# Linear attention and MLP, two layers on one core: TensorE transposes, per-chunk sums of phi(K), one load line and a clock warm-up in the first attention half

## Chip, cores, metric

One core of a Trainium2 chip. The metric is the device time of one execution in microseconds (us), median of several. A profile gives the span of one execution, some 1.8 us less than its time. Engines: PE is TensorE (PEld its weight loads), DVE is VectorE, ACT is ScalarE, POOL is GpSimd, SP is SyncE, which issues transfers. The record calls an execution slow when it is over 1.5% above the fastest of the same kernel, and fast otherwise. Ratios and medians here are of fast executions.

## The reference

```python
def _A_ref(x, wqkv, wo):                      # B,S,D = 1,2048,512; H = 32 heads of 16
    q, k, v = split_heads(x @ wqkv)
    phi = lambda t: jnp.where(t > 0, t + 1, jnp.exp(t)) + 1e-6
    pq, pk = phi(q), phi(k)
    kv = jnp.einsum("bhsd,bhse->bhde", pk, v)
    z = jnp.einsum("bhsd->bhd", pk)
    num = jnp.einsum("bhqd,bhde->bhqe", pq, kv)
    den = jnp.einsum("bhqd,bhd->bhq", pq, z)[..., None] + 1e-6
    return merge_heads(num / den) @ wo
# ... _B_ref: layernorm, gelu(y @ w1 + b1) @ w2 + b2, F = 1792
x = x + _A_ref(_layernorm(x), A_wqkv, A_wo)
x = x + _B_ref(_layernorm(x), B_w1, B_b1, B_w2, B_b2)
# and both once more
```

kv and z are sums over all 2048 tokens. Nothing behind them can start before the last token tile has been normalised, transposed, multiplied and summed.

## The kernel before

Tokens lie in 16 tiles of 128, four to a chunk. The program is a graph of operations. When it is built, a list scheduler walks the graph, gives every engine a fixed order from priorities (`CONF`) and rough durations, and deals out buffers and PSUM banks. Each engine then runs its line strictly in that order, waiting on semaphores. A changed duration or operation can so change the order of everything.

A token tile of the first half: statistics, rstd by a power on POOL, the norm, the transpose by DMA, K, phi, and G = y' phi(K), held in four PSUM banks over all 16 tiles (V's weights are applied later, to G).

```python
G.op("dve", lambda e: e.bn_stats(stats[:, s.slot, :], src()), ...)                       # norm()
G.op("pool", lambda e: e.tensor_tensor(rstd..., veps..., neghalf[:], op=ALU.pow), ...)
G.op("dve", lambda e: e.tensor_scalar(yb[:, y.slot, :], src(), mv..., rstd..., ...), ...)
# ... transpose()
return e.dma_start_transpose(dst, yb[:, y.slot, :])                                      # on SP
# ... attn_k(): four matmuls, then phi() = exp and relu on ACT, min and add on DVE, and
G.op("pool", lambda e: e.tensor_tensor(zacc[:], zacc[:], pkb[:, pk.slot, :], op=ALU.add), 1060, ...)
# ... attn_kv(): z from zacc by four float matmuls, after all 16 tiles
```

Tokens and the K weights are loaded at once from two queues; later weights are each issued from POOL behind the transpose of some tile (tiles 3, 4, 6, 8, 10, 12).

Of the kernel before, what the change touches and what calls it, by code (L numbers as in the profile page):

```python
# [5 lines left out]
FP32 = mybir.dt.float32  # L6
# [4 lines left out]
P = 128  # L11
S = 2048
D = 512
# [97 lines left out]
class Scheduler:  # L111
# [13 lines left out]
    def run(self):  # L125
# [14 lines left out]
        dma_free = {e: 0.0 for e in ENGINES}  # L140
        left = len(g.ops)
        while left:
# [50 lines left out]
            if e == "sp" or o.sem is not None:  # L193
                begin = max(at + 100.0, dma_free[e])
                dma_free[e] = begin + o.nbytes
                o.end = dma_free[e] + o.lat
            else:
                o.end = at + dur + o.lat
# [83 lines left out]
def assign_waits(graph, order, sems, dma_sems):  # L282
# [10 lines left out]
    while len(done) < total:  # L293
# [45 lines left out]
    P_DEN=-26.42, P_A2=-18.03, P_W1=-20, P_W2=60.8, P_K=57.09, P_G=112.94, P_Q=209.56, STEP=4.23, A1_Q=54.88,  # L339
    A1_STEP=0.81, N_H=3, N_N=2, GAP=20.55, TABLE_PENALTY=28.66, WINDOW=199.3,  # L340
    SHIFT={
        "B00": -43.3, "B01": -114.4, "B02": -3.1, "B10": -64.2, "B11": -19.4, "B12": 0.1, "B13": 20.3,
        "D00": -0.8, "D01": -10.8, "D02": 12.4, "D03": -7.8, "D10": -47.3, "D11": -25.2, "D12": 14.0,
        "D13": -11.5, "G00": 37.6, "G01": -77.2, "G02": -29.0, "G03": -10.1, "G11": -54.7, "G12": 12.0,
        "G13": 2.7, "K00": -55.0, "K01": -125.9, "K02": 2.5, "K03": 5.1, "K10": -18.4, "K11": 18.2,
        "K12": -110.6, "K13": 7.6, "N00": -105.8, "N01": -6.7, "N10": -103.0, "N11": 102.7, "N12": 20.6,
        "N13": -61.5, "O00": -5.8, "O01": 9.2, "O02": -104.5, "O03": -191.9, "O10": -61.1, "O11": -27.2,
        "O12": -8.3, "O13": -95.1, "Q00": -5.3, "Q01": -8.6, "Q03": 3.2, "Q11": 7.5, "Q13": -17.6,
        "U00": -69.9, "U01": -24.5, "U02": -15.0, "U03": 4.7, "U10": -72.1, "U11": -2.2, "U12": -137.9,
        "U13": -0.4, "V0": 4.1, "V1": 1.7, "W00": 20.4, "W01": 9.8, "W02": 39.8, "W03": 14.4, "W10": 3.7,  # L350
        "W11": -12.6, "W12": 7.1, "W13": -1.0,
# [4 lines left out]
def build_kernel(nc, A_x, A_wqkv, A_wo, B_x, B_w1, B_b1, B_w2, B_b2, out, conf=None, report=False):  # L356
# [5 lines left out]
    with ExitStack() as es:  # L362
# [14 lines left out]
        id16 = SB("id16", [16, 16], BF16)  # L377
# [28 lines left out]
        def bank(t, n=512):  # L406
# [17 lines left out]
            "g4": ((0,), 1),  # L424
            "n": ((6, 7, 5, 4, 3, 2, 1, 0), cf["N_N"]),
# [6 lines left out]
        def dma(eng, fn, writes, tiles=(), reads=(), prio=0.0, name="", kb=0, sem=None, after=(), transpose=False):  # L432
            sem = sem or f"d_{name}"
            if sem not in dma_names:
                dma_names.append(sem)
            busy = 1300.0 if transpose else 100.0 + kb * 1024 / 230.0
            return G.op(eng, fn, 950.0 if eng == "pool" else 100.0, reads=reads, writes=writes, tiles=tiles, prio=prio,
                        name=name, lat=1000.0 if transpose else DMA_LAT, sem=sem, nbytes=busy, after=after)
# [6 lines left out]
        wsrc = A_wqkv.rearrange("(dt p) c -> p dt c", p=P)  # L445
        for k in range(4):
            dma("sp", lambda e, k=k: e.dma_start(x0ap(0, k), x_dram[k * P:(k + 1) * P, :]), [("x0", k)], [x0[0]],
                prio=-100 + k, name=f"x{k}", kb=128)
            if k == 0:
                dma("act", lambda e: e.dma_start(wqkv[:, :, D:2 * D], wsrc[:, :, D:2 * D]), ["wk"], prio=-99.5, name="wk", kb=512)  # L450
        for c in range(1, NC):
            dma("act", lambda e, c=c: e.dma_start(
                t4[:, x0[c].slot, :].rearrange("p (k d) -> p k d", k=4),
                x_dram[c * 512:(c + 1) * 512, :].rearrange("(k p) d -> p k d", p=P)),
                [("x0", 4 * c + k) for k in range(4)], [x0[c]], prio=-90 + c, name=f"xc{c}", kb=512)

        G.op("pool", lambda e: e.memset(neghalf[:], -0.5), 100, writes=["neghalf"], prio=-100)
        G.op("pool", lambda e: e.memset(eps6[:], 1e-6), 100, writes=["eps6"], prio=-97)
        wq_dma = dma("pool", lambda e: e.dma_start(wqkv[:, :, 0:D], wsrc[:, :, 0:D]), ["wq"], prio=-99, name="wq", kb=512)
        G.op("pool", lambda e: e.memset(ones32[:], 1.0), 100, writes=["ones32"], prio=-98)  # L460
        G.op("pool", lambda e: e.memset(id16[:], 1.0), 100, writes=["id16"], prio=-98)
        G.op("pool", lambda e: e.affine_select(id16[:], id16[:], pattern=[[1, 16]], compare_op=ALU.is_equal, fill=0.0,
                                               base=0, channel_multiplier=-1), 200, reads=["id16"], writes=["id16"], prio=-97)
        b1_dma = dma("sp", lambda e: e.dma_start(b1r[:], B_b1.rearrange("(ft p) -> ft p", p=P)), ["b1r"], prio=-80, name="b1", kb=4)
        dma("sp", lambda e: e.dma_start(b2b[:], bass.AP(B_b2.tensor, B_b2.offset, [[0, P], [1, D]])),
            ["b2b"], prio=-79, name="b2", kb=128)

# [3 lines left out]
        def consts(prio, after):  # L471
            G.op("pool", lambda e: e.memset(onesm[:], 1.0), 500, writes=["onesm"], prio=prio, after=after)
            G.op("pool", lambda e: e.affine_select(bdmask[:], onesm[:], pattern=[[0, DT], [-16, 8], [0, 16]],
                                                   compare_op=ALU.is_ge, fill=0.0, base=0, channel_multiplier=1),
                 900, reads=["onesm"], writes=["bdmask"], prio=prio)
            G.op("pool", lambda e: e.affine_select(bdmask[:], bdmask[:], pattern=[[0, DT], [16, 8], [0, 16]],
                                                   compare_op=ALU.is_ge, fill=0.0, base=15, channel_multiplier=-1),
                 900, reads=["bdmask"], writes=["bdmask"], prio=prio)
# [42 lines left out]

        def yTa(yT):
# [14 lines left out]
        def attn_k(L, c, k, yT, prio):  # L537
# [13 lines left out]
            phi(b, f"k{L}_{st}", lambda: pkb[:, pk.slot, :], f"pk{L}_{st}", [pk], prio, f"k{L}_{st}")  # L551
            if st == 0:
# [7 lines left out]
        def attn_q(L, c, yT, pq, prio):  # L560

            G.grp = f"Q{L}{c}"
            for kt in range(DT):
# [9 lines left out]
                phi(b, f"q{L}_{c}_{kt}", lambda kt=kt: yTa(pq)[:, kt, :], f"pq{L}_{c}_{kt}", [pq], prio + 0.8 * kt, f"q{L}_{c}_{kt}")  # L573

# [51 lines left out]
        def attn_kv(L, prio):  # L626

            G.grp = f"V{L}"
            zt = Tile(psum, f"zb{L}", "g")
            b = Tile(psum, f"kv{L}", "g")  # L630

            def zfn(e):
                for kt in range(DT):
                    ins = e.matmul(bank(zt)[:, kt:kt + 1], lhsT=zacc[:, kt * P:(kt + 1) * P], rhs=ones32[:, :], start=True, stop=True)
                return ins
            G.op("pe", zfn, 900, reads=["zacc", "ones32"], writes=[f"zp{L}"], tiles=[zt], prio=prio, name=f"Z{L}", lat=MM_DRAIN, n=8)

            def fn(e):
                for kt in range(DT):
                    for dc in range(DT):  # L640
# [6 lines left out]
                                                  bank(zt)[:, 0:DT].unsqueeze(2).broadcast_to([P, DT, P]), op=ALU.mult), 640,  # L647
                 reads=[f"zp{L}", "bdmask"], writes=["zb"], tiles=[zt], prio=prio, name=f"zb{L}", lat=40)
# [40 lines left out]
        def mlp_front(L, c, k, yT, prio, on_act):  # L689
# [3 lines left out]
            transpose(y, ykey, yT, k, f"yB{L}_{st}", prio, f"B{L}_{st}")  # L693
# [21 lines left out]
        def mlp_down(L, c, k, g, prio, last):  # L715
# [14 lines left out]
            else:  # L730
# [9 lines left out]
        G.op("pe", lambda e: e.matmul(bank(b1b)[:, 0:FT], lhsT=b1r[:, :], rhs=id16[0:FT, 0:FT], start=True, stop=True), 200,  # L740
             reads=["b1r", "id16"], writes=["b1p"], tiles=[b1b], prio=-60, name="b1T", lat=MM_DRAIN)
# [4 lines left out]
        for c in range(NC):  # L746
            yT = Tile(T4, f"yT0_{c}")
            pq = Tile(T4, f"pq0_{c}")
            pq1.append(pq)
            for k in range(4):  # L750
# [4 lines left out]
                tr = transpose(y, ykey, yT, k, f"yT0_{st}", pr, f"A0_{st}")  # L755
                pk = attn_k(0, c, k, yT, pr + 3)
                attn_g_held(0, st, k, y, ykey, pk, gb, pr + 6)
                if st == 3:
                    late("wv", "wv", wqkv[:, :, 2 * D:3 * D], wsrc[:, :, 2 * D:3 * D], pr, 512, [tr])
                if st == 4:  # L760
                    late("wo", "wo", wo[:], A_wo.rearrange("(dt p) c -> p dt c", p=P), pr, 512, [tr])
                if st == 5:
                    consts(pr, [tr])
                if st in (6, 8):
                    h = (st - 6) // 2
                    late(f"w1_{h}", f"w1_{h}", w1[:, 2 * h:2 * h + 2, :], B_w1.rearrange("(dt p) c -> p dt c", p=P)[:, 2 * h:2 * h + 2, :],
                         pr, 896, [tr])
                if st in (10, 12):
                    h = (st - 10) // 2
                    late(f"w2_{h}", f"w2_{h}", w2[:, 7 * h:7 * h + 7, :], B_w2.rearrange("(ft p) c -> p ft c", p=P)[:, 7 * h:7 * h + 7, :],  # L770
                         pr, 896, [tr])
            attn_q(0, c, yT, pq, -60 + A1S * (4 * c + 3) + cf["A1_Q"])
        attn_g_out(0, gb, -10)
        attn_kv(0, -10)
# [4 lines left out]
        for L in range(2):  # L779
# [35 lines left out]
            if L == 0:  # L815
                attn_kv(1, NC * PERIOD)
# [90 lines left out]
```

## Time and profile before

| | before |
|---|---|
| time, median of 3 (range) | 370.57 us (367.44 to 370.70) |
| span of the profile | 367.5 us |
| first K matmul / last G / first MLP-up matmul | 13.3 / 62.9 / 89.0 us |

Three rows of the page: first the busy time of each engine; then, with the span in 40 slices of 9.2 us, PE's busy share and its granted clock, each digit in tenths.

```profile
PE 325.9 (89%) x1468; PEld 145.6 (40%) x1497; DVE 224.9 (61%) x506; ACT 236.5 (64%) x364; POOL 121.1 (33%) x147
...
PE   0579478775999999999999999997999999998996
...
PEclk9999789996999999999999999998999999999999
```

PE's low digits and the low granted clock lie in the first ten slices: the first attention half and the way to the first MLP. By the working in the prediction they hold about three quarters of the loss, 38.9 of 51.1 us. I keep its names: stretch 1 is up to the first K matmul, stretch 2 from there to the last G, stretch 3 to the first MLP-up matmul, stretch 4 the rest.

### The profile page before, as it was taken

How to read it: one execution, taken by the hardware profiler on the slowest of the kernel's cores; microseconds unless marked ns; L12 is line 12 of the kernel's file. 1: busy time of each engine (PE TensorE's matmuls, PEld its weight loads, DVE VectorE, ACT ScalarE, POOL GpSimd, SP SyncE). 2: the span in 40 equal slices, each digit the busy share in tenths (PEclk: the TensorE clock that was granted, in tenths of full speed). 3: DMA queues.
4: the chain of work that ended last, by engine and by line, in shares of the span. 5: the costliest groups of instructions: out<-in, count | busy, mean ns of one | idle time of the engine just before them, and what ended most of it. 6: DMA issues, size and time to landing. Idle time of an engine off the chain costs nothing.

```text
span 367.5 us, 4243 instructions
## 1 busy us (share of the span) xinstructions
PE 325.9 (89%) x1468; PEld 145.6 (40%) x1497; DVE 224.9 (61%) x506; ACT 236.5 (64%) x364; POOL 121.1 (33%) x147
## 2 busy tenths in 40 slices
PE   0579478775999999999999999997999999998996
PEld 0233134331444444444444444442444444443442
DVE  2689797887089927684075769998852472361022
ACT  1445256986897999799924349896797468514600
POOL 2378573052045534173031534016610070070000
PEclk9999789996999999999999999998999999999999
DMA  8646990011012220021101120002110031021011
GB/s 255 159 128 159 174 226 2 0 30 29 0 30 43 43 45 15 14 45 28 29 3 29 29 45 14 0 4 57 31 28 29 0 85 31 0 71 45 0 45 43
DMA packets 41201, 18.77 MB, mean 51 GB/s; under 512 B 35356, under 2 KB 40092, under 8 KB 41180
## 3 DMA queue, kind: packets, MB, share of 16 engines
q1 hardware_dynamic: 37868, 11.15, 15.1%
q0 software_dynamic: 1200, 5.24, 4.8%
q10 hardware_dynamic: 2112, 2.10, 1.8%
q8 instruction: 12, 0.20, 0.2%
q14 instruction: 9, 0.07, 0.1%
HBM read 8.00 MB, written 2.10 MB: 27 GB/s over the span
## 4 chain that ended last, share of the span: by engine, by line
PE 67%; DMA 10%; DVE 9%; ACT 7%; POOL 4%; issue 2%; SPq 0%; DVEq 0%
PE ps L722 25%; PE ps L704 23%; DMA t<-yb 9%; PE ps L682 6%; PE ps L546 5%; PE ps L610 3%; DVE yb L508 2%; PE ps L568 2%; POOL rstd L496 2%; DVE eb L532 2%; POOL xsb L694 2%; ACT lr L667 1%; ACT gT L710 1%; PE ps L665 1%; DMA t<-in_A_x_dram 1%
## 5 line engine op out<-in xcount | busy, mean ns | idle before, releaser
L704 PE MATMUL ps<-t,w 128*128 128x512 bf16 x436 | 100.4, 383 | 2.0 <-DMA t<-yb 0.9
L722 PE MATMUL ps<-w,gT 128*128 128x512 bf16 x442 | 99.3, 379 | 0.7 <-ACT gT L710 0.3
L710 ACT ACTIVATE gT<-ps,b1c 128x512 bf16<-128x512 f32 x112 | 73.7, 688 | 21.9 <-PE ps L704 21.6
L496 POOL TENSOR_TENSOR rstd<-veps,neghalf 128x1 f32<-128x1 f32 x64 | 37.3, 588 | 143.4 <-DVE veps L490 104.9
L704 PEld LDWEIGHTS ps<-t,w 128*128 128x128 bf16 x448 | 44.0, 99 | 56.2 <-issue 2.7
L722 PEld LDWEIGHTS ps<-w,gT 128*128 128x128 bf16 x448 | 43.7, 98 | 53.5 <-ACT gT L710 0.8
L528 ACT ACTIVATE eb<-ps 128x512 bf16<-128x512 f32 x64 | 38.2, 601 | 34.5 <-PE ps L546 24.9
L532 DVE TENSOR_SCALAR eb<-eb 128x512 bf16<-128x512 bf16 x64 | 27.3, 428 | 35.5 <-ACT eb L528 34.9
L556 POOL TENSOR_TENSOR zacc<-zacc,pkb 128x512 f32<-128x512 f32 x30 | 36.2, 1206 | 36.3 <-DVE pkb L534 25.0
L546 PE MATMUL ps<-wqkv,t 128*128 128x512 bf16 x127 | 34.8, 412 | 13.4 <-DMA t<-yb 13.3
L694 POOL TENSOR_TENSOR xsb<-xsb,b2b 128x512 f32<-128x512 f32 x32 | 38.8, 1222 | 15.2 <-ACT yb L503 6.3
L530 ACT ACTIVATE rb<-ps 128x512 bf16<-128x512 f32 x64 | 38.4, 602 | 6.9 <-PE ps L546 6.9
L503 ACT ACTIVATE yb<-xsb,nmr,rstd 128x512 bf16<-128x512 f32 x24 | 19.4, 813 | 28.5 <-DVE nmr L500 28.5
L843 ACT ACT_TABLE_LOAD x28 | 35.9, 1283 | 0.5
L682 PE MATMUL ps<-gtb,t 128*128 128x512 bf16 x126 | 31.6, 394 | 4.9 <-DVE t L671 2.3
L485 DVE BATCH_NORM_STATS2 stats<-xsb 128x6 f32<-128x512 f32 x48 | 33.1, 690 | 0.9
L732 DVE TENSOR_TENSOR outb<-ps,xsb 128x512 bf16<-128x512 f32 x16 | 11.1, 691 | 34.0 <-PE ps L722 34.0
L568 PE MATMUL ps<-t,wqkv 128*128 128x512 bf16 x124 | 31.2, 387 | 0.2
L667 ACT ACTIVATE lr<-ps,eps 128x512 f32<-128x512 f32 x32 | 21.7, 677 | 8.2 <-PE ps L665 4.5
L671 DVE TENSOR_TENSOR t<-t,lr 128x512 bf16<-128x512 bf16 x32 | 22.3, 700 | 7.2 <-ACT lr L669 7.1
L686 DVE TENSOR_TENSOR xsb<-ps,xsb 128x512 f32<-128x512 f32 x16 | 10.7, 682 | 24.7 <-PE ps L682 24.7
L546 PEld LDWEIGHTS ps<-wqkv,t 128*128 128x128 bf16 x128 | 12.7, 104 | 32.2 <-DMA t<-yb 12.5
(54 smaller groups left out, 268.6 us busy)
## 6 DMA issues: line engine op xcount, KB each, us to landing
w<-in_B_w_dram POOLq DMA_DIRECT2D x4, 896.0 KB, 7.0
out_dram<-outb SPq DMA_DIRECT2D x16, 128.0 KB, 1.7
t<-in_A_x_dram ACTq DMA_DIRECT2D x3, 512.0 KB, 9.4
wqkv<-in_A_wqkv_dram POOLq DMA_DIRECT2D x2, 512.0 KB, 6.3
t<-yb SPq DMA_TRANSPOSE x64, 2.4
wqkv<-in_A_wqkv_dram ACTq DMA_DIRECT2D x1, 512.0 KB, 4.2
t<-in_A_x_dram SPq DMA_DIRECT2D x4, 128.0 KB, 5.7
wo<-in_A_wo_dram POOLq DMA_DIRECT2D x1, 512.0 KB, 3.8
```

What stands on the lines that cost most here:

```text
L496: G.op("pool", lambda e: e.tensor_tensor(rstd[:, s.slot:s.slot + 1], veps[:, s.slot:s.slot + 1], neghalf[:], op=ALU.pow), 570, reads=[k + ...
L528: G.op("act", lambda e: e.activation(eb[:, et.slot, :], bank(bt), ACT.Exp), 500, reads=[src_key], writes=[f"e{tag}"], tiles=[bt, et], prio ...
L530: G.op("act", lambda e: e.activation(rb[:, rt.slot, :], bank(bt), ACT.Relu), 500, reads=[src_key], writes=[f"r{tag}"], tiles=[bt, rt], pri ...
L546: ins = e.matmul(bank(b), lhsT=yTa(yT)[:, dt, k * P:(k + 1) * P], rhs=wqkv[:, dt, D:2 * D], start=(dt == 0), stop=(dt == DT - 1))
L556: G.op("pool", lambda e: e.tensor_tensor(zacc[:], zacc[:], pkb[:, pk.slot, :], op=ALU.add), 1060, reads=[f"pk{L}_{st}", "zacc"], writes=[" ...
L568: ins = e.matmul(bank(b), lhsT=wqkv[:, dt, kt * P:(kt + 1) * P], rhs=yTa(yT)[:, dt, :], start=(dt == 0), stop=(dt == DT - 1))
L682: ins = e.matmul(bank(wb), lhsT=yTa(pq)[:, kt, k * P:(k + 1) * P], rhs=gtb[:, kt, :], start=(kt == 0), stop=(kt == DT - 1))
L694: G.op("pool", lambda e: e.tensor_tensor(xsb[:, st, :], xsb[:, st, :], b2b[:], op=ALU.add), 1060, reads=[("x", st), "b2b"], writes=[("x", ...
L704: ins = e.matmul(bank(b), lhsT=w1[:, dt, ft * P:(ft + 1) * P], rhs=yTa(yT)[:, dt, :], start=(dt == 0), stop=(dt == DT - 1))
L710: G.op("act", lambda e, ft=ft, b=b: e.activation(gT[:, g.slot, ft * 512:(ft + 1) * 512], bank(b), ACT.Gelu_apprx_tanh, bias=b1c[:, ft:ft + ...
L722: ins = e.matmul(bank(b), lhsT=gT[:, g.slot, ft * 512 + k * P:ft * 512 + (k + 1) * P], rhs=w2[:, ft, :], start=(ft == 0), stop=(ft == FT - 1))
L843: e.preload_act_table_set(sets[table])
```

## The change

The intent: end the waits for DMA transposes by using TensorE for half of the first half's tiles, take the running sum of phi(K) off POOL, set all late loads into one line, and start TensorE's clock early. All priorities were fitted anew.

```diff
+        def transpose_pe(y, ykey, yT, k, key, prio, tag, on_act):   # 4 PE transposes into one PSUM bank, 1 copy on ACT
+                    ins = e.transpose(v()[:, d * P:(d + 1) * P], yb[:, y.slot, d * P:(d + 1) * P], idp[:])
...
-                tr = transpose(y, ykey, yT, k, f"yT0_{st}", pr, f"A0_{st}")
+                if st < cf["N_PT"]:                                  # 8: chunks 0 and 1
+                    tr = transpose_pe(y, ykey, yT, k, f"yT0_{st}", pr, f"A0_{st}", True)
+                else:
+                    tr = transpose(y, ykey, yT, k, f"yT0_{st}", pr, f"A0_{st}")
+                if st == 0:                                          # one line of loads behind tile 0
+                    load_chunk("pool", 2, -90, [tr])
+                    load_chunk("pool", 3, -89, [tr])
+                    late("wv", ...); late("wo", ...); late("w1_0", ...); late("w1_1", ...); late("w2_0", ...); late("w2_1", ...)
...
+        def attn_z(L, c, pks, prio):                                 # after each chunk; no sum on POOL in the first half
+                        ins = e.matmul(bank(b)[:, kt:kt + 1], lhsT=pkb[:, pks[k].slot, kt * P:(kt + 1) * P], rhs=onesm[:, 0:1], ...)
+                G.op("dve", lambda e: e.tensor_tensor(zs[:], bank(b)[:, 0:DT], zs[:], op=ALU.add), ...)
...
+        def warm(e):                                                 # 11 dead matmuls at the start
+                ins = e.matmul(bank(wu), lhsT=onesm[:, 0:P], rhs=onesm[:, :], start=True, stop=True)
...
-            transpose(y, ykey, yT, k, f"yB{L}_{st}", prio, f"B{L}_{st}")
+            if c < cf["N_PB"]:                                       # 1: chunk 0 of both MLP fronts
+                transpose_pe(y, ykey, yT, k, f"yB{L}_{st}", prio, f"B{L}_{st}", True)
...
-    P_DEN=-26.42, P_A2=-18.03, ...            # all priorities replaced; the scheduler's
+    N_PB=1, N_PT=8, P_DEN=-24.74, ...         # durations of loads and of transposes beside them too
```

## The prediction

> **What bounds the kernel now.** I began with the page: TensorE (PE) is 89% busy and the chain that ended last is 67% PE, so the time is PE's work plus PE's lost time. I then cut the span at three events of PE's own timeline: its first K matmul (13.3), the last G matmul of the first attention half (62.9; all 16 token tiles are summed there) and the first MLP-up matmul (89.0). This is the view of busy time in stretches (engine busy, in brackets instructions; then granted clock, DMA share, GB/s):
>
> ```profile
> core 0: us, PE busy (x) PEld busy (x) DVE busy (x) ACT busy (x) POOL busy (x), PEclk, DMA share, GB/s
> 0.00:13.30 13.30, 0.16 (x1) 0.10 (x1) 6.05 (x19) 2.75 (x3) 3.94 (x15) 1.00 0.91 272
> 13.30:62.90 49.60, 38.55 (x153) 15.87 (x157) 39.23 (x86) 23.91 (x46) 31.44 (x37) 0.93 0.62 132
> 62.90:89.00 26.10, 17.70 (x91) 7.97 (x90) 23.22 (x51) 21.97 (x40) 7.45 (x8) 0.93 0.10 21
> 89.00:367.50 278.50, 269.52 (x1226) 121.62 (x1249) 156.38 (x351) 187.90 (x278) 78.28 (x88) 0.99 0.13 29
> ```
>
> PE's busy time hides its losses, so I count weight loads (one per matmul; some matmul records are missing, no load is) and multiply by the pace of an unbroken run. Two lines of the chain of waits give the pace: 3.02 / 14 = 0.216 us for 512 columns, 0.89 / 16 = 0.056 us for 128.
>
> ```profile
> 146.10 3.02 PE ps L722 x14
> 237.54 0.89 PE ps L641 x16
> ```
>
> Work against length: stretch 1, about 0.2 of 13.3, 13.1 lost. Stretch 2, 156 x 0.216 = 33.7 of 49.6, 15.9 lost. Stretch 3, 67 x 0.216 + 0.9 (16 small ones) + 0.8 (the float sums of z) = 16.2 of 26.1, 9.9 lost. Stretch 4, 1225 x 0.216 + 1.7 = 266.3 of 278.5, 12.2 lost. So 316.4 us are work and 51.1 lost, 38.9 of it before 89.0. That is where the change works.
>
> What loses it, from the waits before 89.0 (engine, line, waited for: us in total, times, longest) and the chain of waits (start, us, what):
>
> ```profile
> PE ps L546 <- DMA t<-yb: 13.3, 5, 5.0
> PE ps L665 <- DVE t L534: 5.7, 1, 5.7
> ```
> ```profile
> 6.47 6.80 DMA t<-yb
> ...
> 38.51 4.85 DMA t<-yb
> ...
> 46.53 9.33 DMA t<-yb
> ...
> 82.77 1.37 DVE yb L508
> ```
>
> The reader is to see that PE stands for transposes by DMA of normalised tokens: 6.8 us for the first, 4.85 and 9.33 for two while weights load. In quiet stretches one lands in 2.4 us. The second limit is VectorE (DVE): 39 of 49.6 and 23 of 26.1 us busy. Part of that is not its own. Groups before 88 us by form (count | busy, mean ns):
>
> ```profile
> L532 DVE TENSOR_SCALAR eb<-eb 128x512 bf16<-128x512 bf16 x27 | 11.2, 417 | 6.4 <-ACT eb L528 6.2
> L534 DVE TENSOR_TENSOR pkb<-eb,rb 128x512 bf16<-128x512 bf16 x16 | 9.9, 621 | 1.1 <-ACT rb L530 0.7
> L508 DVE TENSOR_SCALAR yb<-t,mv,rstd 128x512 bf16<-128x512 bf16 x16 | 9.7, 617 | 2.8 <-POOL rstd L496 2.4
> L534 DVE TENSOR_TENSOR t<-eb,rb 128x512 bf16<-128x512 bf16 x11 | 8.1, 732 | 0.3
> L556 POOL TENSOR_TENSOR zacc<-zacc,pkb 128x512 f32<-128x512 f32 x15 | 17.4, 1159 | 7.3 <-DVE pkb L534 6.6 <-DVE veps L494 0.4
> ```
> ```profile
> 49.88 0.43 DVE L534 TENSOR_TENSOR pkb<-eb,rb 128x512 bf16<-128x512 bf16 x1
> ...
> 50.38 1.15 POOL L556 TENSOR_TENSOR zacc<-zacc,pkb 128x512 f32<-128x512 f32 x1 [1.35 <-DVE pkb L534]
> ...
> 50.54 1.28 DVE L534 TENSOR_TENSOR pkb<-eb,rb 128x512 bf16<-128x512 bf16 x1
> ```
>
> The same addition takes 0.43 us alone and 1.28 us under GpSimd's (POOL's) running sum of phi(K).
>
> **What the Trainium skill says.** (1) "SBUF — State Buffer", Who interferes with whom: DVE and GpSimd share one SBUF port pair as an exclusive lock, and a DVE op with two SBUF inputs blocks against a GpSimd op that reads SBUF. The 0.43 against 1.28 us agrees. (2) "TensorE: Matmul & The Clock Gate", What's actually happening: PE starts at half clock and needs about 3.4 us of activity to be released. The trace agrees: the first 16 matmuls took 5.49 us where 16 x 0.216 is 3.5, and the eight at 42.97 took 3.59 after 5 idle us. (3) The same page, Part 4: a PE transpose takes about 275 to 390 ns alone and lands in PSUM, so it must be copied out. No row of this trace has one; in a run of four I take the 56 ns of a 128-column matmul, an estimate. (4) "DMA: Bandwidth & Descriptors", Issuing engines are not separate DMA queues: all queues share 16 DMA engines. It agrees: transposes take 2.4 us in quiet and up to 9.3 beside weight loads.
>
> **The change part by part.**
> Transposes: tiles 0 to 7 of the first half, and the four of chunk 0 in each of the two MLP fronts, go to PE: 16 tiles x 4 x 0.056 = 3.6 us of PE, and 16 copies on ScalarE (ACT) at 0.6 (its PSUM reads of 512 take 0.60) = 9.6 us. ACT has room: 23.9 of 49.6 busy. A tile's path from yb to usable is about 0.4 + 0.6 + hand-overs, say 1.3 us, against 2.4 to 6.8. With yb 0 ready near 6.4, K 0 can start near 8 instead of 13.3: 5 us less lost in stretch 1.
>
> Loads: tokens of chunks 2 and 3 and all late weights (2 x 0.5 + wv 0.5 + wo 0.5 + 4 x 0.9 MB = 5.6 MB) are issued back to back from POOL once tile 0 is transposed, near 8 us. Eight issues x 0.85 (rows of 0.72 to 0.99) block POOL, and with it the rstd powers, until about 15. At the 330 GB/s that the DMA view shows in its fullest slices they land by about 26, so the DMA transposes of tiles 8 to 15 meet an idle fabric: 2.4 us each, not 4.85 and 9.33.
>
> Sums: 15 POOL additions and a cast, 18.0 us, go; 64 one-column matmuls come, bound by their weight loads at some 0.056 = 3.6 us, less the 0.8 of the old ones. DVE gets back: 27 minima x (0.417 - 0.29) = 3.4, 16 norms x (0.617 - 0.40) = 3.5, 16 x (0.621 - 0.43) + 11 x (0.732 - 0.43) = 6.4; together 13.3 us, most of it before 62.9.
>
> Clock: 11 warm-up matmuls x 0.427 = 4.7 us in idle time at the start, so the first K run goes at full clock: 5.49 - 3.5 = 2.0, and with no 5-us gaps the 1.9 at 43 is saved too.
>
> **Sum for stretch 2.** DVE needs per tile 0.61 + 0.21 + 0.15 + 0.38 for the norm and 0.70 for phi = 2.05, times 16 = 33 us, plus some six Q phis at 0.70 = 4, from 3.25 on with some 3 us of early gaps: 43. PE needs 128 x 0.216 = 27.6, transposes 1.8, sums 3.6, 24 Q matmuls 5.2: 38 from 8 on, 46 at best. Add some 4 us for the POOL block, which holds back tiles 2 and 3, and for handovers: the last G near 50 instead of 62.9, 13 us earlier. Stretch 3 is a chain (G copies, KV, M, copies, denominators, four norms with 1.16 us bias additions and 0.55 us powers on POOL): I shorten it from 26 to 24, for PE transposes and the early z; the first MLP-up matmul comes near 74. That is 15 off. Stretch 4 pays some 1.1 for transposes. The new priorities may fill part of its 12.2 lost us, such as the wait at 330 to 334 for the last chunk's transposes, or open others; I credit nothing net but the 1.1. So I take 15 off 370.6 for 355.6, and shade to 355 for the filling.
>
> **Rivals.** First: DVE stays the bound and the loss only changes its releaser. For it: DVE is busy 23 of 26 us in stretch 3, where no running sum blocks it, and 4 Q tiles per chunk remain. Against: 13.3 us of DVE time in stretch 2 are pure blocking. It would give about 7 off, 363. Second: the load burst moves the wait. POOL is held for 7 us, rstd comes late, x tiles 8 to 15 and wv arrive behind each other, and PE waits at 10 to 17 us as long as before. For it: POOL is in order and the burst stands ahead of the powers. Against: only tiles 2 to 7 are touched, and DVE has statistics to do meanwhile. It costs 5 of the 15: 360. Third: the schedule later absorbs it. MLP of chunk 0 starts early, but norms, Q and denominators of later chunks are not ready and PE gaps open at 75 to 100; for it, ACT is busy at 0.84 in stretch 3 and switches tables at 1.28 us each. It would leave 8 off, 362. Fourth, upward: the PE floor. 316.4 + 3.6 + 2.8 + 1 of handovers is 324; with 8 us of start, 12.2 late and only 6 elsewhere, the kernel would take 350 of span, 352 timed, and with the late gaps filled 346.
>
> **Range and chances.** The three ways down end at 360 to 363, the way up at 346 to 352; each change removes a measured loss from the chain, and none adds over 4 us to PE. Eight in ten: 346 to 362. Two per cent is 363.2. Faster 0.90, within 0.08, slower 0.02.
>
> **What would show it.** Right: first K matmul at 7 to 9 us; longest PE wait for a transpose under 3 us; the DVE additions of phi at about 0.43 in the first half; the granted clock 1.00 up to the last G, near 50; the first MLP-up matmul at 71 to 77; stretch 4 as long as before within 4 us. Wrong: a new PE wait on ACT copies or on rstd at 9 to 17 us; phi still slow, so that POOL's sum was not the cause; the first MLP-up at 74 but a span over 362, which would mean that the gain was given back later.

## The result

| | before | after |
|---|---|---|
| time, medians | 369.0 us (4 runs) | 356.65 us (4 runs) |
| ratio | | 0.9664 (0.9597 to 0.9731) |
| profiled span | 367.5 | 353.8 |
| stretch 1 | 13.3 | 7.1 |
| stretch 2 | 49.8 | 49.0 |
| stretch 3 | 25.9 | 18.6 |
| stretch 4 | 278.5 | 279.1 |

A ratio is the mean time of one kernel's fast runs over that of the other's of the same rounds, so it is not quite the ratio of the medians. In this table and below the last G is taken at the end of its last matmul, 63.1 before. The changed kernel was run again as a control on another chip: 0.9666.

The same rows of the page, after:

```profile
PE 332.0 (94%) x1628; PEld 150.1 (42%) x1628; DVE 216.0 (61%) x511; ACT 239.4 (68%) x376; POOL 103.2 (29%) x131
...
PE   6786998969989998999999999999999999999996
...
PEclk9998999989999999999999999999999999999999
```

Busy time in stretches, cut at the changed kernel's own events:

```profile
0.00:7.06 7.06, 4.86 (x16) 1.83 (x16) 2.96 (x8) 1.92 (x3) 3.38 (x13) 1.00 0.75 226
7.06:55.90 48.84, 40.84 (x254) 18.94 (x254) 34.22 (x107) 31.26 (x59) 14.71 (x23) 0.97 0.56 154
55.90:74.70 18.80, 13.77 (x84) 6.50 (x83) 16.83 (x37) 16.80 (x33) 6.98 (x8) 0.98 0.01 1
74.70:353.80 279.10, 272.57 (x1276) 122.83 (x1276) 162.02 (x361) 189.46 (x284) 78.11 (x89) 1.00 0.12 27
```

The total came as predicted, 356.65 us for 355, and so did the first MLP-up matmul, 74.7 for "near 74". (The saving is smaller than predicted, 12.4 us by the medians for 15.6: the prediction started from 370.6, the median of three, and four runs put the kernel before at 369.0.) But stretch 2 is hardly shorter, and stretch 3 gave what stretch 2 did not. Two errors cancelled, and the experiments are about them.

What filled stretch 2 is in PE's timeline (start, length, engine, line, instruction, count, idle time before and its releaser) and in one line of the chain of waits:

```profile
24.26 0.54 PE L630 MATMUL ps<-onesm,pkb 128*128 128x1 bf16 x16
29.87 1.89 PE L591 MATMUL ps<-wqkv,t 128*128 128x512 bf16 x4 [5.07 <-DMA t<-yb]
31.55 5.24 PE L647 MATMUL ps<-pkb,yb 128*128 128x512 bf16 x20
```
```profile
20.80 9.03 DMA t<-yb
```

Tile 8 is the first whose transpose is still a DMA. It was issued at 20.80, while the load line was running, and landed at 29.87, 9.03 us later; the last of the line's loads was issued at 16.2 and landed 12.4 us later, at 28.6. PE stood 5.07 us, and the first K group behind the gap took 1.89 us instead of 1.04: the clock had fallen.

DVE's groups in the first 75 us show that the sums no longer block it:

```profile
L577 DVE TENSOR_SCALAR eb<-eb 128x512 bf16<-128x512 bf16 x25 | 8.1, 328 | 6.2 <-ACT eb L573 6.1
L579 DVE TENSOR_TENSOR pkb<-eb,rb 128x512 bf16<-128x512 bf16 x16 | 6.7, 423 | 1.5 <-ACT rb L575 1.2
L529 DVE TENSOR_SCALAR yb<-t,mv,rstd 128x512 bf16<-128x512 bf16 x16 | 6.6, 422 | 1.3 <-POOL rstd L517 0.9
```

The additions went from 621 to 423 ns, the norms from 617 to 422, the minima from 417 to 328.

Stretch 3 in two pieces, cut at the first output projection (72.83 before, 62.26 after). First before, then after:

```profile
62.90:72.83 9.93, 7.81 (x51) 4.16 (x51) 9.24 (x20) 9.45 (x19) 0.00 (x0) 1.00 0.00 0
72.83:89.00 16.17, 9.89 (x40) 3.81 (x40) 13.98 (x31) 12.52 (x22) 7.45 (x8) 0.89 0.16 33
```
```profile
56.10:62.26 6.16, 4.66 (x34) 2.45 (x34) 5.63 (x13) 6.13 (x13) 0.00 (x0) 1.00 0.00 0
62.26:74.70 12.44, 8.92 (x51) 4.05 (x50) 11.00 (x26) 10.47 (x20) 6.98 (x8) 0.97 0.01 2
```

DVE and ACT are nearly full in the first piece in both kernels. After, they have 13 and 13 instructions in it instead of 20 and 19. PE's timeline shows five denominator matmuls (z times phi(Q)) between 48.8 and 55.1, before the last G; before the change the first came at 66.3, after it.

### The profile page after: what moved, and what is told of

It is laid out like the page before. It is cut to its first block, busy times and chain, and to the rows that moved or that the text cites. A ratio compares the mean times of both kernels' runs of the same rounds, so it can differ in the third digit from the quotient of the medians.

```text
span 353.8 us, 4505 instructions
## 1 busy us (share of the span) xinstructions
PE 332.0 (94%) x1628; PEld 150.1 (42%) x1628; DVE 216.0 (61%) x511; ACT 239.4 (68%) x376; POOL 103.2 (29%) x131
## 4 chain that ended last, share of the span: by engine, by line
PE 58%; DVE 11%; issue 10%; POOL 7%; ACT 7%; DMA 6%; ACTq 0%; DVEq 0%; POOLq 0%
PE ps L795 22%; PE ps L777 22%; DMA t<-yb 4%; PE ps L591 4%; PE ps L752 4%; POOL rstd L517 4%; DVE yb L529 3%; POOL xsb L767 3%; DVE stats L506 3%; PE ps L615 2%; PE ps L677 2%; DMA t<-in_A_x_dram 2%; ACT gT L783 2%; ACT lr L737 2%; ACT yb L524 2%
## 5 line engine op out<-in xcount | busy, mean ns | idle before, releaser
L783 ACT ACTIVATE gT<-ps,b1c 128x512 bf16<-128x512 f32 x112 | 74.6, 687 | 27.0 <-PE ps L777 26.7
L767 POOL TENSOR_TENSOR xsb<-xsb,b2b 128x512 f32<-128x512 f32 x32 | 38.6, 1210 | 16.2 <-ACT yb L524 9.8
L591 PE MATMUL ps<-wqkv,t 128*128 128x512 bf16 x128 | 32.4, 387 | 7.8 <-DMA t<-yb 6.0
L575 ACT ACTIVATE rb<-ps 128x512 bf16<-128x512 f32 x64 | 39.2, 612 | 0.0
L577 DVE TENSOR_SCALAR eb<-eb 128x512 bf16<-128x512 bf16 x64 | 20.4, 320 | 24.7 <-ACT eb L573 24.5
L741 DVE TENSOR_TENSOR t<-t,lr 128x512 bf16<-128x512 bf16 x32 | 23.5, 738 | 8.5 <-ACT lr L739 8.5
L603 POOL TENSOR_TENSOR zacc<-zacc,pkb 128x512 f32<-128x512 f32 x15 | 18.0, 1201 | 24.1 <-DVE pkb L579 22.0
L529 DVE TENSOR_SCALAR yb<-xsb,mv,rstd 128x512 bf16<-128x512 f32 x24 | 18.0, 748 | 7.0 <-POOL rstd L517 6.2
```

The costliest lines, as they stand in the source:

```text
L575: G.op("act", lambda e: e.activation(rb[:, rt.slot, :], bank(bt), ACT.Relu), 500, reads=[src_key], writes=[f"r{tag}"], tiles=[bt, rt], pri ...
L591: ins = e.matmul(bank(b), lhsT=yTa(yT)[:, dt, k * P:(k + 1) * P], rhs=wqkv[:, dt, D:2 * D], start=(dt == 0), stop=(dt == DT - 1))
L767: G.op("pool", lambda e: e.tensor_tensor(xsb[:, st, :], xsb[:, st, :], b2b[:], op=ALU.add), 1060, reads=[("x", st), "b2b"], writes=[("x", ...
L783: G.op("act", lambda e, ft=ft, b=b: e.activation(gT[:, g.slot, ft * 512:(ft + 1) * 512], bank(b), ACT.Gelu_apprx_tanh, bias=b1c[:, ft:ft + ...
```

## The experiments

Most experiments hold the order: each engine runs the operations that both versions have in exactly the order of the kernel that it is compared with, and a new operation gets the place of the one it stands for. Without this, the scheduler would reorder the whole kernel, and stretches 3 and 4 would move for other reasons. Buffers and PSUM banks are dealt anew. In the traces, the instructions of DVE and ACT come in the same order as in the kernel compared with, but for the added and removed ones. All twelve runs gave correct results. Lines of code (L...) differ between versions; the operation names do not.

### A control: the changed kernel again

The second group of runs, on another chip, has its own control, the changed kernel with no edit.

> The changed kernel once more, as the control for the other three on the same chip: 0.966 of the time before, within 0.005; last G at 55 to 57, first MLP-up matmul at 74 to 76 us.

Measured: 357.64 us, ratio 0.9666 (0.9614 to 0.9719), as expected; last G 57.0, first MLP-up 75.6, stretch 3 18.6 again. Its granted clock was 0.66 from 10 to 15 us, where the first profile had lost none, and 0.50 from 30 to 35 us, behind tile 8's wait, where the first had 0.69. So where and how far the clock drops varies from one execution to another; the last G of the two profiles differs by 0.9 us.

### GpSimd's sums put back, beside TensorE's

```diff
             if L == 0:
+                G.op("pool", lambda e: e.tensor_tensor(zacc[:], zacc[:], pkb[:, pk.slot, :], op=ALU.add), ...)   # result unused
                 return pk
```

> The changed kernel with every engine's order held, and the 16 running sums of phi(K) put back on GpSimd as dead work (nothing of the first half reads them; TensorE still makes the sums). It gives back the port lock alone. My theory: phi additions of the first half rise from 0.42 to over 0.6 us and minima from 0.33 to over 0.4, the last G of the first half slips from 55.9 to 59 to 62, and the span grows by 3 to 6 us. Rival: VectorE has slack in that stretch (34 of 49 us busy), so the additions are slower but the last G and the span move by less than 1.5 us.

Measured: 365.49 us, ratio 0.9938; last G 64.1 instead of 56.1, stretch 3 18.8, stretch 4 280.1. The cost is 0.9938 - 0.9664 = 0.027 of the time before, some 10 us, more than I expected. DVE's groups:

```profile
L749 DVE TENSOR_TENSOR pkb<-eb,rb 128x512 bf16<-128x512 bf16 x16 | 10.1, 635 | 0.3
...
L699 DVE TENSOR_SCALAR yb<-t,mv,rstd 128x512 bf16<-128x512 bf16 x16 | 8.0, 497 | 8.5 <-POOL rstd L687 8.1
```

Additions at 635 ns: the block is back. But DVE also idles 8.1 us for rstd instead of 0.9, because the powers stand behind the sums in POOL's line. Two costs, and the next experiment parts them.

### GpSimd kept as busy, without reading

The edit is shown against lock_back:

```diff
-                G.op("pool", lambda e: e.tensor_tensor(zacc[:], zacc[:], pkb[:, pk.slot, :], op=ALU.add), ...)
+                G.op("pool", lambda e: e.memset(scratch[:], 0.0), ...)      # 128x1260 bf16: 1164 ns
```

> As lock_back, but GpSimd's dead work only writes (a store of about the same length, which reads nothing that VectorE's additions need). It keeps GpSimd's line as full and takes away the block on two-input additions. lock_back put the last G at 64.1. If the time went through GpSimd's own line (rstd powers behind the sums), last G stays at 60 to 64; if it went through blocked additions on VectorE, phi additions are back at 0.42 us and last G at 56 to 58.5.

Measured: 359.34 us, ratio 0.9734 beside the control's 0.9666 in the same rounds.

```profile
L748 DVE TENSOR_SCALAR eb<-eb 128x512 bf16<-128x512 bf16 x24 | 10.3, 432 | 1.2 <-ACT eb L744 1.1
L700 DVE TENSOR_SCALAR yb<-t,mv,rstd 128x512 bf16<-128x512 bf16 x16 | 7.2, 451 | 9.0 <-POOL rstd L688 8.7
L750 DVE TENSOR_TENSOR pkb<-eb,rb 128x512 bf16<-128x512 bf16 x16 | 6.6, 417 | 0.6 <-ACT rb L746 0.3
```

The additions are free again at 417 ns while POOL is as full, and the waits for rstd stay (8.7 us). The minima, which have one input, are still slowed: 432 against 328. By the times, the full line, with the minima that its stores slow, costs 0.0068 x 370 = 2.5 us, and the reading some 7.5 of the 10. The 7.5 compares two groups of rounds, but the intervals are far apart (0.9857 to 1.002 for lock_back, 0.9680 to 0.9788 here). The 2.5 is likely and not certain: the control's interval, 0.9614 to 0.9719, overlaps this one, though only one of its six times is above the fastest here. By the profile the parts look more even (last G 61.4), but the profiled run was the slowest of its six, 362.15 us, so I go by the times: the blocked additions are shown to count, and they count more.

### No warm-up

```diff
-        G.op("pe", warm, 11 * 427, reads=["onesm"], ...)
```

> The changed kernel, order held, without the 11 warm-up matmuls. My prediction's step says 2.0 us of stretch 2: the first K matmuls run at half clock, some 0.43 us each, and the last G slips by 1 to 2 us. Rival: TensorE waits for VectorE and for data between 7 and 18 us anyway, so slower matmuls there only eat waits: last G and span within 0.7 us.

Measured: 352.93 us over the three fast runs (a fourth, 357.5, was slow), ratio 0.9586; last G 54.3, earlier than with the warm-up. Neither theory said that. The timeline has the reason:

```profile
29.62 1.04 PE L759 MATMUL ps<-wqkv,t 128*128 128x512 bf16 x4 [2.43 <-DMA t<-yb]
30.50 4.48 PE L815 MATMUL ps<-pkb,yb 128*128 128x512 bf16 x20
```

Without the warm-up everything up to tile 8 is later, and its transpose is issued at 23.19 instead of 20.80. It lands at 29.62 instead of 29.87: it seems to wait for the end of the load line either way, whose last load lands at 28.3 here and at 28.6 there. PE stands 2.43 us instead of 5.07, the clock holds, and the K group takes 1.04 us and the next twenty matmuls 4.48, where the changed kernel took 1.89 and 5.24. The warm-up saved its two microseconds and lost them at the load line, with the clock on top. The intervals of 0.9586 and 0.9664 overlap, so I claim no more than that it brought nothing here.

A caution on the clock column: in this run it reads 1.00 up to 15 us, though the K groups at 6.91 and 11.52 took 1.89 us each. Near the start, the matmuls' own times are the surer sign.

### Tiles 0 to 7 by DMA again

```diff
-    N_PB=1, N_PT=8, ...
+    N_PB=1, N_PT=0, ...         # and the load line starts behind the norm of tile 0, so at the same place
```

> The changed kernel, order held, tiles 0 to 7 of the first half transposed by DMA again (chunk 0 of the MLP fronts stays with TensorE); the late loads start at the same place as in the changed kernel. My theory: the transposes run beside the load burst, take 4 to 9 us each, first K near 12, several TensorE waits of 3 us and more, last G 6 to 12 us later than 55.9, span 6 to 10 us longer. Rival: VectorE sets the pace and catches up: first K late, but last G within 2 us.

Measured: 372.9 us, ratio 1.013 (1.006 to 1.020), a little slower than the kernel before. First K 10.5, last G 74.2 (18 us later, where I expected 6 to 12), stretch 3 18.6, stretch 4 278.6. PE's waits before 95 us:

```profile
PE ps L761 <- DMA t<-yb: 23.2, 7, 11.3
```

Seven waits, 23.2 us in all, the longest 11.3; one transpose took 18.3 us to land. The rival, that DVE sets the pace, falls. The load line without the transposes by TensorE costs 0.047, some 17 us. Whether the line pays at all beside them is not shown; the next experiment, which moves most of it, is faster.

### w1 and w2 issued after the last transpose of the half

```diff
-                if st == 0: ... late("w1_0", ..., [tr]) ... late("w2_1", ..., [tr])
+                if st == ST - 1: late("w1_0", ..., [tr]) ... late("w2_1", ..., [tr])   # tr: transpose of tile 15
```

> The changed kernel, order held but for this: the four loads of w1 and w2 (3.6 MB of the 5.6 MB burst) are issued only after the last DMA transpose of the first half has landed. My theory: the wait of 5.07 us for tile 8 and the half clock after it come from the burst; the transpose then lands in 2.4 to 4 us, the wait falls under 2 us, last G comes 4 to 6 us earlier (50 to 52) and the first MLP-up matmul 3 to 5 us earlier. Rival: stretch 3 is set by VectorE and ScalarE (16.8 of 18.8 us busy each), so an earlier last G only lengthens it: first MLP-up within 1.5 us of 74.7, span within 1.5 us.

Measured: 351.81 us, ratio 0.9559 (0.9488 to 0.9629; this touches the changed kernel's 0.9597 to 0.9731, but its times, 350.74 to 352.79, all lie below 355.55 to 357.47); last G 52.8, first MLP-up 71.4, stretch 3 18.6 again. PE's waits for transposes fall from 5.1 to 0.2 us; the longest landing is 4.0 us:

```profile
PE ps L761 <- DMA t<-yb: 0.2, 1, 0.2
```

The edit also takes 3.5 us of issuing out of POOL's line, ahead of the rstd powers. That is not where the gain comes from: from the first K matmul to the last z sums before tile 8 no_warmup takes 19.7 us and the run without warm-up below, with the loads moved, 19.6.

The rival falls: an earlier last G is passed on whole. But this profile lost its clock at another place, in the gap after the first K group (10 to 15 us, the columns as above, clock third from the end):

```profile
10.00:15.00 5.00, 4.25 (x15) 1.77 (x16) 4.62 (x17) 1.76 (x4) 3.29 (x6) 0.50 0.94 337
```

### The same without warm-up, and with more of it

```diff
-        G.op("pe", warm, 11 * 427, reads=["onesm"], ...)      # on top of the edit of the loads above
```

> late_w12 without the warm-up matmuls. My reading of no_warmup: the warm-up does save 2.4 us up to tile 8, but that is waited away at the load burst, which ends near 30 us either way; and the longer wait then drops the clock. With the burst moved, the warm-up should be worth 1 to 3 us again: last G at 53.5 to 56 against 52.8. But late_w12's own profile shows half clock from 10 to 15 us, warm-up or not, so if the clock falls in that gap anyway the two are within 0.7 us (rival).

Measured: 351.14 us, ratio 0.9502 (0.9459 to 0.9545); last G 51.7. So even with the loads out of the way, eleven warm-up matmuls brought nothing that can be told from noise: late_w12's interval is 0.9488 to 0.9629. The profiled executions suggest why: with the clock lost again, late_w12's K group at 11.47 took 1.89 us, as long as the one at 11.16 without a warm-up.

And with dead matmuls in two more places, the first warm-up kept:

```diff
+                    # dead matmuls on TensorE: 7 behind the first K group, 2 behind tile 1's transposes
+                    G.op("pe", bridge, 1.0, reads=["onesm"], ...)
```

> late_w12 with nine more dead matmuls on TensorE: seven in its idle time after the first K group (8.3 to 9.7 us), two behind the second tile's transposes. They keep the clock up in the gap where late_w12 lost it. Theory: granted clock 1.00 to the last G, tile 8 reached 2 to 3 us earlier, last G 50 to 51.5, span 348 to 349.5. Rival: VectorE's pace takes over (its norms and phi are busy 16 of 18 us there), last G within 1 us of 52.8.

Measured: 349.5 us, ratio 0.9463 (0.9418 to 0.9509), the fastest version; its profile:

```profile
6.75:50.30 43.55, 41.42 (x263) 19.24 (x263) 33.78 (x107) 31.43 (x60) 14.73 (x23) 1.00 0.55 174
```

The clock is 1.00 to the last G at 50.3 and stretch 2 is 43.6 us with PE busy 41.4 of them. Beside the control of the same rounds (0.9666) the loads and the filling together are worth 2%. Against late_w12_no_warmup alone the gain is 0.4% with overlapping intervals: a likely gain, not a shown one.

### Chunk 0 of the MLP fronts by DMA again

```diff
-    N_PB=1, N_PT=8, ...
+    N_PB=0, N_PT=8, ...
```

> The changed kernel, order held, with the transposes of chunk 0 of both MLP fronts by DMA again. Stretch 3 (last G to first MLP-up) was 25.9 us before and is 18.6 now; I had given it 24. My reading: 2.5 to 4 of those 7.3 us are this part, since from the end of the last normalised tile to the first MLP-up matmul it took 4.9 us before and takes 1.1 now. Expected: last G unchanged, stretch 3 at 21 to 22.5 us, span 3 to 6 us longer with the second layer's. Rival (all of stretch 3 is the new priorities): stretch 3 within 0.7 us of 18.6.

Measured: 361.14 us, ratio 0.9797, so this part is worth 0.013, or 4.8 us by the times (0.9753 to 0.9841, clear of the changed kernel's interval). It is spread thinner than expected: stretch 3 is 20.0, only 1.4 more, and stretch 4 is 281.6, some 2.5 more (the second layer). The last G was 58.4 in this profile, 2.3 later, from a wait of 6.8 us for tile 8's transpose, which the edit does not touch. PE's waits, for tile 8 and before the first MLP-up matmul:

```profile
PE ps L761 <- DMA t<-yb: 6.8, 1, 6.8
PE ps L947 <- DMA t<-yb: 6.3, 1, 6.3
```

My reading, that the fronts make up 2.5 to 4 us of stretch 3's gain, falls, and so does the rival, that they make up nothing. What is left, some 6 of 7.3 us, goes with the order; no run isolates it.

### Parts alone in the kernel before

```diff
+            attn_z(0, c, pks, pr + 6)     # sums of phi(K) by TensorE; POOL's out (its memset of ones goes to DVE)
```

> The kernel before, its order held, with one part alone: sums of phi(K) by TensorE per chunk. If GpSimd's sums were what set the time (lock_back cost 8 to 10 us), last G comes 4 to 8 us earlier than 63.1. If the waits for DMA transposes (13.3 us) set it, VectorE's gain is waited away and last G is within 2.5 us. Stretch 3 stays at 25.9 within 1 us.

Measured: 369.26 us, ratio 1.0007. The first half did gain: last G 58.8 (4.3 us earlier), first MLP-up 84.3 instead of 89.0, stretch 3 25.5. Stretch 4 gave it all back, 282.8 for 278.5. ACT's timeline and PE's show where the largest part of it went:

```profile
94.33 1.28 ACT L1050 ACT_TABLE_LOAD   x1
95.63 0.60 ACT L706 ACTIVATE eb<-ps 128x512 bf16<-128x512 f32 x1
96.24 1.28 ACT L1050 ACT_TABLE_LOAD   x1
```
```profile
98.28 1.78 PE L907 MATMUL ps<-t,w 128*128 128x512 bf16 x4 [2.87 <-ACT gT L913]
```

PE's next group for the MLP waits 2.87 us for a gelu that stands behind a pair of table loads around one exp. In the kernel before the same exp stood in the same place of ACT's line and no such wait is in the trace. As banks were dealt anew, the group may wait for another gelu than it did, so I do not claim that every insertion of this part would lose there. What is shown is that a gain in the first half reaches the end only if the order behind it can take it.

The same with tiles 0 to 7 transposed by TensorE as well:

```diff
-                tr = transpose(y, ykey, yT, k, f"yT0_{st}", pr, f"A0_{st}")
+                if st < 8:
+                    tr = transpose_pe(y, ykey, yT, k, f"yT0_{st}", pr, f"A0_{st}", True)
+                else:
+                    tr = transpose(y, ykey, yT, k, f"yT0_{st}", pr, f"A0_{st}")
```

> The kernel before, its order held, with two parts: sums by TensorE and tiles 0 to 7 transposed by TensorE; loads, warm-up, MLP fronts and priorities as before. My sum for stretches 1 and 2 was 13 us for all parts; these two should bring most of it: first K at 8 to 9, last G at 50 to 56, span 356 to 361. Stretch 3 stays at 25.9 within 1 us, since its gain came from the new order and the fronts. Rival (the new priorities and the load line matter most): last G later than 59.

Measured: 369.82 us, ratio 1.0033; first K 12.0, last G 59.4, stretch 3 25.5, stretch 4 282.8. My expectation failed. The held order was the reason for the late first K: PE's line begins with the transpose of b1, which waits 10.6 us for its load, and PE's transposes stand behind it. Waits for DMA transposes did fall, to 3.1 us, but the additional PE transposes brought nothing over before_z, and the rest gave back the same 4.3 us.

### The new priorities alone in the kernel before

```diff
-    P_DEN=-26.42, P_A2=-18.03, ...
+    P_DEN=-24.74, P_A2=-36.03, ...
```

> The kernel before with the new priorities alone: every engine's order is worked out again from them. Both sets of priorities were fitted to their own kernels, so I expect no gain: 0.98 to 1.04 of the time before. If the priorities by themselves carried the change, it is below 0.98.

Measured: 385.84 us, ratio 1.0452, somewhat outside the range I gave. The new priorities are worth nothing by themselves. Stretch 3 is 28.0 in its profile, so they do not shorten that alone either, although three denominators run before the last G here too (at 69.4 and 70.8, the last G at 72.0). Two of the parts on the old order give 1.00, the new priorities on the old parts 1.045, and both together 0.966.

## Why the prediction was right, and where its steps were not

- **Start.** "K 0 can start near 8": 7.1. The mechanism is right, for some 3.4 of the 6.2 us: dma_transposes puts the first K at 10.5. The other 2.8 came with the rest of the change (loads at the start, order), which the step does not name.
- **Loads.** "They land by about 26, so the DMA transposes of tiles 8 to 15 meet an idle fabric: 2.4 us each". This step failed. The line ended at 28.6. Tile 8's transpose was issued at 20.8, before that, and took 9.03 us; PE waited 5.07. The line moved the collision from tiles 0 to 7 to tile 8. late_w12 removes the wait.
- **Clock.** "The 1.9 at 43 is saved too" failed: the wait for tile 8 dropped the clock (0.69 of full from 30 to 35 us). The warm-up did what the step says to the first K group (1.04 us, against 1.89 in no_warmup), but its 2.0 us did not reach the end: no_warmup was not slower.
- **Sums.** The mechanism was right, with its size short. lock_back cost some 10 us, of which the blocked reads some 7.5 and POOL's full line, which the sum had left out, likely some 2.5. Sixteen one-column matmuls take 0.54 us in the timeline and one of them 0.163, so a further one costs (0.54 - 0.163) / 15 = 25 ns, not 56.
- **Sum for stretch 2.** "The last G near 50": 56.1. This term was mis-sized: the stretch took 49.0 us for the 42 predicted. With loads and clock mended it took 43.6 with the last G at 50.3, so the sum had counted the work about rightly. It missed the wait for tile 8 (5.1 us) and the clock lost behind it (1.89 + 5.24 instead of 1.04 + 4.48, so 1.6 us).
- **Stretch 3.** "From 26 to 24": 18.6. The reasons named, TensorE transposes and the early z, are too small as sized: front_dma gives 1.4 us to the first. The rest goes with the order: all seven held variants of the changed kernel that left the fronts alone have 18.6 to 18.8, whether the last G is at 50 or 74, and both held variants of the kernel before have 25.5, with PE's wait of 5.7 us for DVE's t still there (5.8). What in the new order does it stays open. Neither the early z in the old order (before_z: 0.4 us gained) nor denominators before the last G (before_priorities ran three, and has 28.0) shortens it alone.
- **Stretch 4.** "1.1 more": 0.6 more.
- **Rivals.** The first, that DVE stays the bound, did not come true: in late_w12_bridge PE is busy 41.4 of the 43.6 us of stretch 2, DVE 33.8. The second, that the load burst moves the wait, was the right one, at another tile and with a size of some 5 us. The third, that the schedule absorbs the gain, did not happen in the changed kernel, but it is what before_z shows. The fourth, with less lost than predicted, gave 346 to 352; late_w12_bridge came to 349.5 once the loads were moved out of the way.

The prediction held because 6.2 off stretch 1, 0.8 off 2 and 7.3 off 3 add to nearly the same as 5, 8 and 2. That is luck: nothing in the prediction argues for the 7.3, and without those 5 extra us the time would have been near 362, the end of the range.

## What to carry to other kernels

A line of large loads is not free for work that waits for a DMA meanwhile: move every load that is not needed soon behind the last transpose, and look at when each transpose lands, not at the mean. An engine that adds on the side can block another through shared ports and through its own in-order line; put back a copy that only fills the line to tell the two apart. In a kernel with a fixed order, measure a part with the order held, and read stretches: taking the sums off POOL was worth 10 us in the new order and nothing at the end in the old one.

## What the Trainium skill lacked or had wrong

- "DMA: Bandwidth & Descriptors", DMA Transpose (X-bar): no figure for how long a transpose takes beside loads. Here one landed in 2.4 us in quiet, 9.03 beside the load line, and up to 18.3 when eight of them met it.
- "TensorE: Matmul & The Clock Gate", Part 4: some 390 ns for a transpose in isolation, 275 in one kernel. A group of eight takes 0.61 to 0.65 us in the trace where one of four takes 0.39 or 0.40, so each further one costs 55 to 65 ns; the section has no figure for a run of them.
- The same page, Why this matters for your kernels: warming up with at least 4 us of matmuls. Eleven of them, 4.0 to 4.9 us, did warm it (first K group 1.04 us, without them 1.89), but that did not last: in late_w12 the clock was 0.50 from 10 to 15 us and in the control 0.66. The idle gaps before were under 2 us each; not counting transposes and the 0.19-us matmul of b1 as work, the gap in late_w12 is 3.0 us (8.5 to 11.5). Which of the two matters no run here shows; nine more matmuls kept the clock at 1.00 in the one profile taken.
- "SBUF — State Buffer", Who interferes with whom: agrees in full. Two-input additions are blocked by a sum that reads (635 ns) and not by a store (417 ns), one-input minima by the store too (432 against 328). It does not say that the in-order line of the sharing engine costs as well: 8.1 us of waits for rstd here.
